# Query features turned by VectorE's 32x32 block transposes in place of TensorE transposes, in an attention-and-GLU block

## The chip, the cores and the metric

One Trainium2 chip, one of its cores. The metric is the device time of one execution in microseconds, the median of several runs. PE is TensorE (its weight loads are shown as PEld), DVE is VectorE, ACT is ScalarE, POOL is GpSimd, and SP is the queue from which this kernel issues all its DMAs. L123 is line 123 of the kernel before.

## The reference

```python
def _A_ref(x, wqkv, w_phi, wo):                 # S 2048, D 1024, H 32 heads, Dh 32
    qkv = (x @ wqkv) -> q, k, v per head
    pq = einsum("bhsd,hdf->bhsf", q, w_phi);  pk the same from k
    phi_q = concat([softmax(pq), softmax(-pq)], -1)      # 64 features a head
    phi_k = concat([softmax(pk), softmax(-pk)], -1)
    kv = einsum("bhsf,bhsd->bhfd", phi_k, v);  z = einsum("bhsf->bhf", phi_k)
    num = einsum("bhqf,bhfd->bhqd", phi_q, kv)
    den = einsum("bhqf,bhf->bhq", phi_q, z)[..., None] + 1e-6
    return (num / den) -> (B, S, D) @ wo

def _B_ref(x, w_gate, w_up, w_down):            # F 3584
    return (sigmoid(x @ w_gate) * (x @ w_up)) @ w_down

xn = layernorm(x)
return x + _A_ref(xn, ...) * silu(_B_ref(xn, ...))
```

Everything is float32.

## The kernel before

A float32 product is made of three matmuls on two-part operands: `split` (L120) copies a tile's rounded part on ACT (L122) and subtracts it on DVE (L123), and `mm3` (L125) issues the three matmuls (L127, L128, L129). Big products go through a 2x2 block scheme with seven products instead of eight; the seven are named B11, B21, T2, T3, T4, T1, B22, and their operands are sums of blocks made on POOL.

The program runs in this order: layer norm and transposes of x; the projections to v, k and q (w_phi is folded into the q and k weights by `fold`); the gate and up products of the GLU, with the key features, the key-value sums and half of the query features in their background; the GLU's down product; then attention and the output product. Token tiles have 128 rows, so there are 16 (TT); heads come in two halves of 512 columns (`hb`, HB).

The query features go through memory three times. `features` (L398) makes exp of the shifted values for both signs from one [128, 512] tile of q, so `e` is [128 tokens, 1024 features] with columns ordered head, sign, feature. For the first eight token tiles `q_features` (L554) does this early and stores `e` in `e_d` and its reciprocal sums in `r_d`; for the other eight `q_task` (L562) does it itself. `q_task` runs 32 times during the down product, popped from `late` in its loop (L926 to L931). It multiplies `e` by the broadcast key sums (POOL, L573), reduces to the denominator (DVE, L576 to L584), scales `e` in place (POOL, L585) and stores it in `e_d` again with one DMA of 512 KB (L586).

In the last stage the scaled features are needed with features on partitions. `e_load` (L612) reads one [128, 1024] tile back into slot 47 or 48 (u is 0 or 1). `phi_transpose` (L618) does four TensorE transposes of 128x128 into one PSUM bank (L623), then splits the bank into two-part operands (ACT reads the bank first, then DVE), and after the second quarter of a tile calls `e_load` for the next one. `numerator` (L632) multiplies by the key-value blocks, copies the result (ACT, L641), and `o_operands` (L648) makes the seven operands of the output product: three copies and four differences on POOL (L653, L656, L657, L661), each then split. `attend` (L665) lists for a pair of token tiles 8 `phi_transpose` and 4 `numerator` calls. Pair 0 is spread over the end of the down product; pair p+1 is spread over the 28 k-steps of pair p's output product (loop at L976), whose results leave the PSUM bank by L992 (ACT) and L994, L996, L1003, L1006 (DVE), are multiplied by the gate and added to x (POOL, L1007 and L1008), and are stored (L1009); `gx_load` (L965) then loads the next gate and x tiles (L970, L971).

The output weights are made into operands by `wo_prep` (L603): load, split, through a ring of two half slots. Those of T1, T4 and B22 come last, when the down product frees its slots.

The order of instructions on each engine is the program order as changed by a planner that follows a timeline model and by the `issue_after` blocks. All DMAs sit on SP in one order, and an SP entry that waits holds what is behind it. PSUM has eight banks: in the last stage two are for transposes (`tpr`), two for numerators (`nmr`), four for the output product (`amm`).

Of the kernel before, what the change touches and what calls it, by code (L numbers as in the profile page):

```python
# [9 lines left out]
F32 = mybir.dt.float32  # L10
F32R = mybir.dt.float32r
AF = mybir.ActivationFunctionType
ALU = mybir.AluOpType
AX = mybir.AxisListType
# [3 lines left out]
P = 128  # L18
S, D, H, DH, F = 2048, 1024, 32, 32, 3584
KT = D // P  # L20
TT = S // P
NCH = 2
CT = S // NCH
CTT = CT // P
NF = F // P
NJ = NF // 2
HB = 512
EPS_LN = 1e-5
EPS_DEN = 1e-6
Q, K, V, O = 0, 1, 2, 3  # L30
# [18 lines left out]
def hedgehog_glu_kernel(  # L49
# [11 lines left out]
    nc = tc.nc  # L61
# [4 lines left out]
    dram = ctx.enter_context(tc.tile_pool(name="dram", bufs=1, space=DRAM))  # L66

    ident = sb.tile([P, P], F32, name="ident")
# [2 lines left out]
    wf_d = dram.tile([4, 7, P, 4, HB], F32, name="wf_d")  # L71
    qkv_d = dram.tile([3, TT, 2, P, HB], F32, name="qkv_d")
    xo_d = dram.tile([7, P, 4, HB], F32, name="xo_d")
    e_d = dram.tile([TT, 2, P, 2 * HB], F32, name="e_d")
    r_d = dram.tile([CTT, 2, P, 32], F32, name="r_d")
    zb_d = dram.tile([2, P, 2 * HB], F32, name="zb_d")
    kvbd_d = dram.tile([4, P, 2, HB], F32, name="kvbd_d")
    ws_d = dram.tile([2 * NJ, 4, P, 2 * HB], F32, name="ws_d")
# [27 lines left out]
    def whole(i):  # L106
        return slots[i].rearrange("p a n -> p (a n)")

    def halves(*ids):
        return [slots[i][:, a] for i in ids for a in range(2)]  # L110

    def run(i, n):

        name, k = where[i]
        return blocks[name][0][:, k:k + n]

    def pair(i):
        return slots[i][:, 0], slots[i][:, 1]

    def split(o, src):  # L120

        nc.scalar.copy(o[0], src)  # L122
        return nc.vector.tensor_sub(o[1], src, o[0].bitcast(F32))  # L123
# [94 lines left out]
    def w_sums(which, k, a11, a12, a21, a22):  # L218
        def keep(i, b):
            nc.sync.dma_start(wf_d[which, i, :, k], b)  # L220

        if which != O:
            for i, b in ((B11, a11), (B21, a12), (T4, a22)):
                keep(i, b)
        nc.gpsimd.tensor_add(a22, a21, a22)
        nc.gpsimd.tensor_sub(a21, a11, a21)
        nc.gpsimd.tensor_sub(a11, a22, a11)
        nc.gpsimd.tensor_sub(a12, a12, a11)
        for i, b in ((T2, a11), (T3, a21), (T1, a22), (B22, a12)):
            keep(i, b)  # L230
# [29 lines left out]
    def fold(which, k):  # L260

        bs = halves(*fblock[which].next())
        for b, (f, h) in zip(bs, ((0, 0), (0, 1), (1, 0), (1, 1))):
            r = fraw.next()
            nc.sync.dma_start(r, wqkT[which, f, k + 4 * h].rearrange("p g n -> p (g n)"))
            ps = tps.next()
            for g in range(4):
                gs = slice(g * P, (g + 1) * P)
                nc.tensor.matmul(ps[:, gs], r[:, gs], bd[:, 4 * f + g], start=True, stop=True)
            nc.scalar.copy(b, ps)  # L270
        w_sums(which, k, *bs)


# [121 lines left out]
            evac(y, u1p[u])  # L395
            store(1, 0, y)

    def features(name, p, e):  # L398

        nh = HB // DH  # L400
        st = small.tile([P, 4, nh], F32, name=f"st{name}", tag="st", bufs=2)
        pv = p.rearrange("p (h d) -> p h d", d=DH)
        mx, mn = st[:, 0], st[:, 1]
        nc.vector.tensor_reduce(mx, pv, axis=AX.X, op=ALU.max)
        nc.vector.tensor_reduce(mn, pv, axis=AX.X, op=ALU.min)
        ev = e.rearrange("p (h t d) -> p h t d", t=2, d=DH)
        nc.vector.tensor_tensor(ev[:, :, 0], pv, mx[:, :, None].to_broadcast([P, nh, DH]), op=ALU.subtract)
        nc.vector.tensor_tensor(ev[:, :, 1], mn[:, :, None].to_broadcast([P, nh, DH]), pv, op=ALU.subtract)
        nc.scalar.activation(e, e, AF.Exp)  # L409
        s2, r2 = [st[:, a:a + 2].rearrange("p t h -> p (t h)") for a in (2, 0)]  # L410
        nc.vector.tensor_reduce(s2, e.rearrange("p (g d) -> p g d", d=DH), axis=AX.X, op=ALU.add)
        nc.vector.reciprocal(r2, s2)
        return r2
# [3 lines left out]
    e_k, zacc = whole(53), whole(54)  # L417
    kvb = banks[4:]
# [60 lines left out]
    def z_broadcast(hb):  # L479

        for i in range(2):
            z = zacc[:, i * HB:(i + 1) * HB]
            a = pair(38)
            split(a, z)
            nc.tensor.matmul(kvb[i], ones, a[0], start=True, stop=False)
            nc.tensor.matmul(kvb[i], ones, a[1], start=False, stop=True)
            nc.scalar.copy(z, kvb[i])
        nc.sync.dma_start(zb_d[hb], zacc)

    def x_task(t):  # L490
        xt = x_load(t, 52)
# [62 lines left out]
    def q_features(t, hb):  # L554

        p, e = qf_raw.next(), whole(qf_e.next())
        nc.sync.dma_start(p, qkv_d[Q, t, hb])
        r = features(f"q{t}{hb}", p, e)
        nc.sync.dma_start(r_d[t, hb], r)
        nc.sync.dma_start(e_d[t, hb], e)  # L560

    def q_task(t, hb):  # L562
        e, ez = whole(eqr.next()), whole(52)
        if t < CTT:
            nc.sync.dma_start(e, e_d[t, hb])
            r = small.tile([P, 32], F32, name=f"r{t}{hb}", tag="r", bufs=2)
            nc.sync.dma_start(r, r_d[t, hb])
        else:
            p = qraw.next()
            nc.sync.dma_start(p, qkv_d[Q, t, hb])  # L570
            r = features(f"q{t}{hb}", p, e)
        st = small.tile([P, 5, 16], F32, name=f"sa{t}{hb}", tag="sa", bufs=2)
        nc.gpsimd.tensor_mul(ez, e, zb)  # L573
        d2 = st[:, 0:2].rearrange("p t h -> p (t h)")
        r2 = st[:, 2:4].rearrange("p t h -> p (t h)")
        nc.vector.tensor_reduce(d2, ez.rearrange("p (g d) -> p g d", d=DH), axis=AX.X, op=ALU.add)  # L576
        nc.vector.tensor_mul(d2, d2, r)
        den = st[:, 4]
        nc.vector.tensor_reduce(den, d2.rearrange("p (h t) -> p h t", t=2), axis=AX.X, op=ALU.add)
        nc.vector.tensor_scalar_add(den, den, EPS_DEN)  # L580
        nc.vector.reciprocal(den, den)
        nc.vector.tensor_mul(r2.rearrange("p (h t) -> p h t", t=2), r.rearrange("p (h t) -> p h t", t=2),
                             den[:, :, None].to_broadcast([P, 16, 2]))
        e3 = e.rearrange("p (g d) -> p g d", d=DH)  # L584
        nc.gpsimd.tensor_mul(e3, e3, r2[:, :, None].to_broadcast([P, 32, DH]))  # L585
        nc.sync.dma_start(e_d[t, hb], e)  # L586

# [22 lines left out]
    def e_load(u):  # L612
        tp_, hb = divmod(e_next[u], 2)
        if tp_ < NTP:
            nc.sync.dma_start(whole(47 + u), e_d[2 * tp_ + u, hb])
        e_next[u] += 1

    def phi_transpose(tp_, u, hb, q):  # L618
        ps = tpr.next()
        e = whole(47 + u)  # L620
        for j in range(4):
            k = 4 * q + j
            nc.tensor.transpose(ps[:, j * P:(j + 1) * P], e[:, k * P:(k + 1) * P], ident)  # L623
        if u == 0:
            b = run(phu.next(), 2).rearrange("p a b n -> p (a b n)")
            units_ph[hb, q] = b.rearrange("p (a k t) -> p a k t", a=2, t=256)
        ph, cs = units_ph[hb, q], slice(u * P, (u + 1) * P)
        split((ph[:, 0, :, cs], ph[:, 1, :, cs]), ps.rearrange("p (k t) -> p k t", t=P))
        if q:
            e_load(u)  # L630

    def numerator(tp_, hb, q):  # L632
        ps = nmr.next()
# [96 lines left out]
    for k in range(4):  # L730
        todo(fold, K, k)
    todo(x_rest)
    for k in range(4):
        todo(fold, Q, k)
# [29 lines left out]
    for n, (kind, c, what, i) in enumerate(ops):  # L764
# [20 lines left out]
        j, s = what  # L785
        u = units.index((c, j, s))
# [29 lines left out]
        else:  # L816
            q = {B21: 0, T1: 3, T4: 2, B22: 1}[i]
            g = gates[q]
# [6 lines left out]
            else:  # L825
                if q == 0:
                    nc.vector.tensor_mul(g, g, bank)
                else:
                    b = u1 if q == 1 else u2
# [76 lines left out]
    for n, (i, j, cs) in enumerate(dsteps):  # L906
        w, hs = dready[n]
        for c in cs:
            for u in range(4):
                p = 4 * c + u  # L910
# [15 lines left out]
        if n and n * 32 // 78 > (n - 1) * 32 // 78 and late:  # L926
            t, hb = late.pop(0)
            if t == 0:
                nc.sync.dma_start(zb, zb_d[hb])
            with tc.issue_after(last_split[0]):  # L930
                q_task(t, hb)  # L931
        if 40 <= n < 56 and n % 2 == 0:
            wo_prep(*divmod((n - 40) // 2, 4))
        if n == ND - 2 * NJ:
            assert not late and len(WO[B21]) == 4
            block("x1", 4, 4, F32R)
            for i in (T3, B21):
                side.extend([lambda i=i, k=k: wo_prep(i, k) for k in range(4)])
            side.extend([lambda u=u: e_load(u) for u in range(2)])
# [21 lines left out]
    def rows(tp_, i):  # L961
        f, u = {B21: (0, 0), T1: (1, 1), T4: (1, 0), B22: (0, 1)}[i]
        return 2 * tp_ + u, slice(f * HB, (f + 1) * HB)
# [12 lines left out]
    for tp_ in range(NTP):  # L976
        nxt = attend(tp_ + 1) if tp_ + 1 < NTP else []
        n = 0
        u1, u2, y11, y21 = [res.next() for _ in range(4)]
        for i in range(7):  # L980
            if i in opening:
                abank[i] = amm.next()
            ps = abank[{B21: B11, T4: T3, B22: T1}.get(i, i)]
            o = [h.rearrange("p (k t) -> p k t", t=P) for h in pair(of[tp_][i])]
# [12 lines left out]
            else:  # L997
                g, xt = gxs.pop((tp_, i))
                t, cols = rows(tp_, i)
# [40 lines left out]
```

## Time and profile before

| | |
|---|---|
| median of 3 runs | 2444.24 us (2442.29 to 2448.07) |
| span of the profiled execution | 2442.7 us |
| PE, DVE, ACT, POOL busy, share of the span | 98%, 71%, 41%, 40% |
| mean granted clock of TensorE | 0.998 |
| DMA | 581.60 MB, mean 238 GB/s |
| first and last TensorE transpose of query features (L623) | 2150.1 us, 2408.0 us |

The profile shows one execution. Beside its span no separate time of that execution is given; the span lies 1.5 us under the median of the runs. Matmuls overlap one another, so a busy PE isn't by itself a PE at its peak: the distance from one matmul's start to the next tells what one costs. In a row of groups stand line, engine, operation, written tile and read tiles, shapes and count, then the busy time with the mean of one in ns, then the engine's idle time just before them with what ended it. In a row of waits stand who waited for whom, the total in us, the times and the longest.

### The profile page before, as it was taken

How to read it: one execution, taken by the hardware profiler on the slowest of the kernel's cores; microseconds unless marked ns; L12 is line 12 of the kernel's file. 1: busy time of each engine (PE TensorE's matmuls, PEld its weight loads, DVE VectorE, ACT ScalarE, POOL GpSimd, SP SyncE). 2: the span in 40 equal slices, each digit the busy share in tenths (PEclk: the TensorE clock that was granted, in tenths of full speed). 3: DMA queues.
4: the chain of work that ended last, by engine and by line, in shares of the span. 5: the costliest groups of instructions: out<-in, count | busy, mean ns of one | idle time of the engine just before them, and what ended most of it. 6: DMA issues, size and time to landing. Idle time of an engine off the chain costs nothing. (4 is left out here: it accounts for less than half of the span.)

```text
span 2442.7 us, 31915 instructions
## 1 busy us (share of the span) xinstructions
PE 2386.8 (98%) x11048; PEld 1979.6 (81%) x11048; DVE 1722.3 (71%) x2261; ACT 1001.9 (41%) x1495; POOL 981.5 (40%) x638
## 2 busy tenths in 40 slices
PE   6999999999999999999999999999999999998998
PEld 4888888888888888888888888888888888877887
DVE  7533567767776688548868888647889998865544
ACT  6432244444444443323433444433443334454332
POOL 4530146566665400004545453543333335314554
PEclk9999999999999999999999999999999999999999
DMA  7874567777776764467888887896666767756554
GB/s 275 278 253 169 186 225 266 251 261 263 259 273 244 259 221 167 175 202 260 285 301 286 270 312 267 280 335 216 216 225 220 241 231 241 239 193 193 182 177 130
DMA packets 231506, 581.60 MB, mean 238 GB/s; under 512 B 30385, under 2 KB 30385, under 8 KB 226737
## 3 DMA queue, kind: packets, MB, share of 16 engines
q1 hardware_dynamic: 231344, 579.57, 69.0%
q8 instruction: 87, 1.43, 0.2%
q14 instruction: 75, 0.61, 0.1%
HBM read 353.76 MB, written 225.71 MB: 237 GB/s over the span
## 5 line engine op out<-in xcount | busy, mean ns | idle before, releaser
L127 PE MATMUL bank<-x,w 128*128 128x512 f32 x2352 | 911.3, 390 | 6.8 <-DVE fb L823 2.7
L128 PE MATMUL bank<-x,w 128*128 128x512 f32 x2352 | 916.2, 390 | 0.4 <-DVE x L123 0.3
L129 PE MATMUL bank<-x,w 128*128 128x512 f32 x2352 | 904.5, 389 | 0.0
L123 DVE TENSOR_TENSOR w<-fa,w 128x512 fp32r<-128x512 f32 (+1 forms) x444 | 436.1, 987 | 143.6 <-ACT w L122 139.2
L122 ACT CAST w<-fa 128x512 fp32r<-128x512 f32 (+1 forms) x444 | 307.6, 698 | 541.7 <-PE bank L128 333.4
L127 PEld LDWEIGHTS bank<-x,w 128*128 128x128 f32 x2352 | 441.1, 188 | 101.6 <-DVE fb L823 4.1
L129 PEld LDWEIGHTS bank<-x,w 128*128 128x128 f32 x2352 | 441.6, 188 | 91.9 <-DVE w L123 0.4
L128 PEld LDWEIGHTS bank<-x,w 128*128 128x128 f32 x2352 | 441.7, 188 | 91.5 <-DVE x L123 1.4
L127 PE MATMUL bank<-w,x 128*128 128x512 f32 x708 | 279.1, 395 | 5.2 <-ACT fc L377 2.1
L129 PE MATMUL bank<-w,x 128*128 128x512 f32 x708 | 278.2, 393 | 5.8 <-DVE x L123 5.8
L128 PE MATMUL bank<-w,x 128*128 128x512 f32 x708 | 277.4, 392 | 0.0
L831 POOL TENSOR_TENSOR fc<-fc 128x512 f32<-128x512 f32 x27 | 43.2, 1599 | 298.6 <-DVE fc L830 292.6
L129 PEld LDWEIGHTS bank<-w,x 128*128 128x128 f32 x708 | 133.9, 189 | 35.4 <-DVE x L123 7.8
L127 PEld LDWEIGHTS bank<-w,x 128*128 128x128 f32 x708 | 134.0, 189 | 34.4 <-ACT x L122 3.0
L128 PEld LDWEIGHTS bank<-w,x 128*128 128x128 f32 x708 | 133.9, 189 | 27.1 <-DVE w L123 0.2
L573 POOL TENSOR_TENSOR fc<-fc 128x1024 f32<-128x1024 f32 x32 | 81.4, 2543 | 179.4 <-ACT fc L409 123.2
L831 POOL TENSOR_TENSOR fb<-fb,fc 128x512 f32<-128x512 f32 x57 | 91.7, 1608 | 133.4 <-DVE fc L830 130.4
L313 POOL TENSOR_TENSOR fb<-fa 128x512 f32<-128x512 f32 x28 | 36.7, 1309 | 249.3 <-DMA fa<-w_gu 129.6
L123 DVE TENSOR_TENSOR w<-fb,w 128x512 fp32r<-128x512 f32 (+1 forms) x114 | 107.3, 941 | 30.7 <-ACT w L122 29.4
L122 ACT CAST w<-fb 128x512 fp32r<-128x512 f32 (+1 forms) x114 | 71.4, 626 | 135.4 <-PE bank L128 90.3
L123 DVE TENSOR_TENSOR x<-fa,x 128x512 fp32r<-128x512 f32 x112 | 112.7, 1007 | 17.4 <-ACT x L122 17.1
L830 DVE TENSOR_TENSOR fc<-fc,bank 128x512 f32<-128x512 f32 x84 | 57.2, 681 | 88.5 <-PE bank L129 74.9
(240 smaller groups left out, 3293.7 us busy)
## 6 DMA issues: line engine op xcount, KB each, us to landing
ws_d<-w SPq DMA_DIRECT2D x112, 512.0 KB, 3.8
w<-ws_d SPq DMA_DIRECT2D x112, 512.0 KB, 5.6
fa<-w_gu SPq DMA_DIRECT2D x84, 512.0 KB, 4.1
fa<-h_d SPq DMA_DIRECT2D x84, 512.0 KB, 4.1
fa<-wf_d SPq DMA_DIRECT2D x32, 1024.0 KB, 5.2
h_d<-fc SPq DMA_DIRECT2D x120, 256.0 KB, 3.6
fc<-e_d SPq DMA_DIRECT2D x48, 512.0 KB, 3.8
fc<-qkv_d SPq DMA_DIRECT2D x80, 256.0 KB, 4.0
```

The lines of the kernel that those rows point to most:

```text
L122: nc.scalar.copy(o[0], src)
L123: return nc.vector.tensor_sub(o[1], src, o[0].bitcast(F32))
L127: nc.tensor.matmul(o, a[0], b[0], start=first, stop=False, **kw)
L128: nc.tensor.matmul(o, a[0], b[1], start=False, stop=False, **kw)
L129: nc.tensor.matmul(o, a[1], b[0], start=False, stop=last, **kw)
L313: nc.gpsimd.tensor_add(s1, a21, a22)
L573: nc.gpsimd.tensor_mul(ez, e, zb)
L830: v = nc.vector.tensor_add(b, u2 if q == 3 else u1, bank)
L831: nc.gpsimd.tensor_mul(g, g, b)
```

## The change

The four TensorE transposes of a quarter tile become one VectorE instruction that transposes every 32x32 block of [128, 512] inside its own quadrant of 32 partitions, from SBUF into the same PSUM bank. A block transpose leaves a block in its quadrant, so the rows that lie in one quadrant must already be one quarter of the features. This is arranged ahead of it. The store of the scaled features goes to a new tensor `f_d` in four DMAs, each from 32 partitions (32 tokens) and scattering four runs of 1 KB per partition, so that a reloaded tile has on partition (quarter of the columns, token in block) the columns (block of tokens, feature). `fold` writes the folded q weights with the heads' order changed, in the ACT copy out of PSUM; `features` writes `e` for queries in the order half, sign, head, feature; the key sums of `z_broadcast` are copied in that order too, into `e_k` instead of in place; the denominators' small operations read by the new order. `e_load` reads whole rows of `f_d`, and stands ahead of the split instead of behind it. `e_d` keeps only the early features of eight tiles.

```diff
-    e_d = dram.tile([TT, 2, P, 2 * HB], F32, name="e_d")
+    e_d = dram.tile([CTT, 2, P, 2 * HB], F32, name="e_d")
     r_d = dram.tile([CTT, 2, P, 32], F32, name="r_d")
+    f_d = dram.tile([TT, 2, 4, DH, 4, 256], F32, name="f_d")
...
@@ fold
-            nc.scalar.copy(b, ps)
+            if which == Q:
+                nc.scalar.copy(b.rearrange("p (a g d) -> p g a d", a=2, d=DH), ps.rearrange("p (g a d) -> p g a d", a=2, d=DH))
+            else:
+                nc.scalar.copy(b, ps)
...
@@ features
-        ev = e.rearrange("p (h t d) -> p h t d", t=2, d=DH)
-        nc.vector.tensor_tensor(ev[:, :, 0], pv, mx[:, :, None].to_broadcast([P, nh, DH]), op=ALU.subtract)
-        nc.vector.tensor_tensor(ev[:, :, 1], mn[:, :, None].to_broadcast([P, nh, DH]), pv, op=ALU.subtract)
+        if query:
+            ev = e.rearrange("p (a t h d) -> p t a h d", a=2, t=2, d=DH)
+            pv, mx, mn = [a.rearrange("p (a h) d -> p a h d", a=2) for a in
+                          (pv, mx[:, :, None].to_broadcast([P, nh, DH]), mn[:, :, None].to_broadcast([P, nh, DH]))]
+        else:
+            ev = e.rearrange("p (h t d) -> p t h d", t=2, d=DH)
+            mx, mn = [a[:, :, None].to_broadcast([P, nh, DH]) for a in (mx, mn)]
+        nc.vector.tensor_tensor(ev[:, 0], pv, mx, op=ALU.subtract)
+        nc.vector.tensor_tensor(ev[:, 1], mn, pv, op=ALU.subtract)
...
@@ z_broadcast
-            nc.scalar.copy(z, kvb[i])
-        nc.sync.dma_start(zb_d[hb], zacc)
+            o = e_k.rearrange("p (q g d) -> p g q d", q=4, d=DH)[:, 4 * i:4 * i + 4]
+            nc.scalar.copy(o, kvb[i].rearrange("p (g q d) -> p g q d", q=4, d=DH))
+        nc.sync.dma_start(zb_d[hb], e_k)
...
@@ q_task (the small operations on d2, den and r2 read by "p (a t h) -> p a h t")
-        nc.sync.dma_start(e_d[t, hb], e)
+        for n in range(4):
+            nc.sync.dma_start(f_d[t, hb, :, :, n].rearrange("q s c -> s q c"),
+                              e[n * DH:(n + 1) * DH].rearrange("s (q c) -> s q c", q=4))
...
@@ e_load
-            nc.sync.dma_start(whole(47 + u), e_d[2 * tp_ + u, hb])
+            nc.sync.dma_start(whole(47 + u), f_d[2 * tp_ + u, hb].rearrange("q s n c -> (q s) (n c)"))
@@ phi_transpose
-        e = whole(47 + u)
-        for j in range(4):
-            k = 4 * q + j
-            nc.tensor.transpose(ps[:, j * P:(j + 1) * P], e[:, k * P:(k + 1) * P], ident)
+        nc.vector.transpose(ps.rearrange("p (g n s) -> p n g s", n=4, s=DH),
+                            whole(47 + u).rearrange("p (n g d) -> p n g d", n=4, d=DH)[:, :, 4 * q:4 * q + 4])
+        if q:
+            e_load(u)
         if u == 0:
...
         split((ph[:, 0, :, cs], ph[:, 1, :, cs]), ps.rearrange("p (k t) -> p k t", t=P))
-        if q:
-            e_load(u)
```

More of the change, by code (lines that the diff above doesn't have):

```diff
@@ L396, in proj_out, with features @@
             store(1, 0, y)
-    def features(name, p, e):
+    def features(name, p, e, query=False):
         nh = HB // DH
@@ L557, in q_features @@
         nc.sync.dma_start(p, qkv_d[Q, t, hb])
-        r = features(f"q{t}{hb}", p, e)
+        r = features(f"q{t}{hb}", p, e, True)
         nc.sync.dma_start(r_d[t, hb], r)
@@ L570, in q_task @@
             nc.sync.dma_start(p, qkv_d[Q, t, hb])
-            r = features(f"q{t}{hb}", p, e)
+            r = features(f"q{t}{hb}", p, e, True)
         st = small.tile([P, 5, 16], F32, name=f"sa{t}{hb}", tag="sa", bufs=2)
@@ L578, in q_task @@
         den = st[:, 4]
-        nc.vector.tensor_reduce(den, d2.rearrange("p (h t) -> p h t", t=2), axis=AX.X, op=ALU.add)
+        by_head = "p (a t h) -> p a h t"
+        nc.vector.tensor_reduce(den.rearrange("p (a h) -> p a h", a=2), d2.rearrange(by_head, a=2, t=2), axis=AX.X, op=ALU.add)
         nc.vector.tensor_scalar_add(den, den, EPS_DEN)
         nc.vector.reciprocal(den, den)
-        nc.vector.tensor_mul(r2.rearrange("p (h t) -> p h t", t=2), r.rearrange("p (h t) -> p h t", t=2),
-                             den[:, :, None].to_broadcast([P, 16, 2]))
+        nc.vector.tensor_mul(r2.rearrange(by_head, a=2, t=2), r.rearrange(by_head, a=2, t=2),
+                             den.rearrange("p (a h) -> p a h", a=2)[:, :, :, None].to_broadcast([P, 2, 8, 2]))
         e3 = e.rearrange("p (g d) -> p g d", d=DH)
         nc.gpsimd.tensor_mul(e3, e3, r2[:, :, None].to_broadcast([P, 32, DH]))
-        nc.sync.dma_start(e_d[t, hb], e)
+        for n in range(4):
+            nc.sync.dma_start(f_d[t, hb, :, :, n].rearrange("q s c -> s q c"),
+                              e[n * DH:(n + 1) * DH].rearrange("s (q c) -> s q c", q=4))
     NTP = TT // 2
```

## The prediction

> **What bounds the kernel now.** I read the page's busy shares first (in the table above: PE far ahead of all others), then busy time by stretch around the transposes, then PE's timeline for what one transpose costs, then the waits. The stretches are A, the end of the down product (pair 0 is turned there); B, from there until the last output weights are ready; C, the loop over the pairs. The last pair follows, without transposes. Columns: length, then busy us of PE, PEld, DVE, ACT, POOL, granted clock, DMA share, GB/s. The second fence is the same table for the transposes' line alone, L623.
>
> ```profile
> 2142.00:2183.00 41.00, 37.83 (x197) 31.07 (x196) 29.52 (x42) 24.04 (x44) 7.20 (x5) 1.00 0.77 255
> 2183.00:2242.00 59.00, 52.12 (x268) 42.17 (x266) 33.52 (x45) 24.85 (x46) 19.94 (x15) 1.00 0.47 146
> 2242.00:2415.00 173.00, 169.75 (x968) 146.04 (x969) 89.16 (x122) 64.27 (x116) 90.34 (x66) 1.00 0.55 177
> ```
> ```profile
> 2142.00:2183.00 41.00, 4.94 (x32) 3.87 (x32) 1.00 0.77 255
> 2183.00:2242.00 59.00, 5.37 (x40) 4.61 (x40) 1.00 0.47 146
> 2242.00:2415.00 173.00, 26.51 (x184) 21.94 (x184) 1.00 0.55 177
> ```
>
> In C PE is busy 169.75 of 173 us at full clock and DVE only 89.16, so PE is the bound there and DVE has half its time free. A and B leave PE idle 3.2 and 6.9 us: something else sets their pace in part. The 256 transposes lie 32, 40 and 184 in A, B and C.
>
> PE's timeline shows a group of four between ordinary 128x512 matmuls:
>
> ```profile
> 2161.12 0.39 PE L128 MATMUL bank<-x,w 128*128 128x512 f32 x1
> 2161.35 0.60 PE L623 MATMUL bank<-ident,fc 128*128 128x128 f32 x4
> 2161.71 0.48 PE L129 MATMUL bank<-x,w 128*128 128x512 f32 x1
> 2162.02 0.40 PE L127 MATMUL bank<-x,w 128*128 128x512 f32 x1
> ```
>
> A matmul normally starts 0.23 us after the one before it (2161.12 to 2161.35). From the group's start to the second matmul behind it is 0.67 us (2161.35 to 2162.02); less one matmul, a group costs 0.44 us of PE.
>
> **The change, part by part.**
>
> *TensorE loses 64 groups:* 64 x 0.44 = 28.2 us of PE time: 8 groups or 3.5 us in A, 10 or 4.4 us in B, 46 or 20.2 us in C. In C it is on the path. In B I count little: PE waits there for operands, and the chain of waits runs through the output weights (load, ACT, DVE, next load), then the load of a gate:
>
> ```profile
> 2222.19 4.82 DMA fc<-wf_d
> 2227.03 0.63 ACT x L122
> 2227.68 0.70 DVE x L123
> 2228.40 3.73 DMA fc<-wf_d
> ...
> 2233.53 3.16 DMA fc<-g_d
> ```
>
> None of this gets shorter, so of B's 4.4 us I take 1. In A I take 0: the operands of the down product pass through DVE, whose 29.52 busy us of 41 grow by eight transposes, and PE already stands idle 3.2 us.
>
> *VectorE gains 64 transposes of 128x512.* The profile has none. The nearest rows are other DVE work of 512 float32 per lane:
>
> ```profile
> L123 DVE TENSOR_TENSOR fb<-bank,fb 128x512 fp32r<-128x512 f32 x32 | 21.9, 685 | 27.5 <-ACT fb L122 27.4
> ...
> L404 DVE TENSOR_REDUCE stk<-fc 128x16 f32<-128x512 f32 x32 | 21.6, 676 | 0.2 <-DMA fc<-qkv_d 0.2
> ...
> L407 DVE TENSOR_TENSOR p<-p,stq 128x512 f32<-128x512 f32 x16 | 22.5, 1408 | 0.0
> ...
> L432 DVE COPY fc<-fc 128x1024 f32<-128x1024 f32 x2 | 2.5, 1234 | 0.0
> ```
>
> The lower end is half the copy of twice the length, 0.62 us; the upper is the slowest row of this shape, 1.41 us. I take 0.69 us: a transpose has one SBUF source, like the reduce at 0.68, and writes as many elements. Then DVE has 89.2 + 46 x 0.69 = 120.9 us in C, which shrinks to about 157: 77% busy, not the bound. In A it has 29.5 + 5.5 = 35.0 of 41.
> [...] No run here shows a transpose on DVE.
>
> *The price of the in-order queue.* DVE now does the transposes ahead of the splits that PE waits for. PE's waits in C:
>
> ```profile
> PE bank L127 <- ACT fa L122: 1.7, 1, 1.7
> PE bank L127 <- ACT fc L992: 1.3, 1, 1.3
> PE bank L623 <- DVE x L123: 0.9, 2, 0.5
> PE bank L129 <- DVE x L123: 0.8, 2, 0.4
> ```
>
> Two of the four are already splits late at the seam between two pairs. I charge one transpose, 0.69 us, at each of six seams: 4.1 us. A load of `e` that comes late would now hold DVE instead of PE, with the evacuations (L994 to L1006) and splits queued behind it; today transposes on PE wait for splits (0.9 us above), not for a load, so I charge nothing more. SP's entry for that load waits for the transpose as before (47.4 us in total, below), and what is behind it (gate loads, output stores) moves with it; moved ahead of the split, it costs nothing.
>
> *The stores.* 32 stores become 128, so SP gets 96 more issues of 0.32 us, 31 us over the 420 us of the stores. The load of a later `e` waits on SP for them:
>
> ```profile
> SPq L615 <- PE bank L623: 47.4, 15, 9.1
> ```
> ```profile
> L586 SPq DMA_DIRECT2D e_d<-fc x32: 319/320/659, 1677.5 to 2095.8; - x32
> ...
> DMA to landing us min/median/max: 2.6/3.9/6.4
> ```
> ```profile
> SPq L565 <- DMA e_d<-fc: 42.5, 15, 4.1
> ```
> ```profile
> ACT x L122 <- DMA fa<-wd_d: 31.5, 15, 5.7
> ```
> ```profile
> PE bank L127 <- DVE fc L895: 0.6, 1, 0.6
> PE bank L127 <- DVE x L890: 0.6, 1, 0.6
> ```
>
> Behind that load stand the down product's own loads, and ACT already waits 31.5 us for them, yet the last two rows are all the waits of PE from 1640 to 2142 us. The prepared steps cover it, so I take 0. Without that cover, one more microsecond a store is 15 us.
>
> *The rest at nothing.* The 16 ACT copies in `fold` (0.586 us each by the next row) write in another order; ACT is idle half the time there. If each doubled, 9.4 us would lie on ACT beside PE. The views in `features`, the denominator and the key sums keep counts and sizes.
>
> ```profile
> L270 ACT COPY fc<-bank x16: 576/586/593, 94.8 to 148.5; 128x512 f32<-128x512 f32 x16
> ```
>
> *Sum:* 0 (A) - 1 (B) - 20.2 + 4.1 (C) = -17.1 us. From the span 2442.7 that is 2425.6; the median of the runs stands 1.5 us above the span, so 2427.
>
> **The rivals.**
>
> *All of it is on the path.* PE's waits move elsewhere and A and B shrink too: 28.2 us, 2416. For it: PE is busy 98% of C. Against it: A and B have idle PE while they wait for loads.
>
> *The pairs keep their pace.* If the loop over pairs is set by a result's way out (DVE, POOL, store, then the copy L992 into the same buffer), a lighter PE only waits longer:
>
> ```profile
> 2330.48 0.59 ACT L992 COPY fc<-bank 128x512 f32<-128x512 f32 x1 [2.29 <-DMA out<-fc]
> ...
> 2388.79 0.59 ACT L992 COPY fc<-bank 128x512 f32<-128x512 f32 x1 [0.61 <-DMA out<-fc]
> ```
>
> Of seven such copies only these two show a wait today, and the first costs PE 1.3 us. If the 3.4 us that PE saves a pair is mostly lost here, 15 us of C's go and 2440 is left. Against it: the other five.
>
> *VectorE becomes the bound (slower).* In C this decides when 89.2 + 46X passes 173, at X = 1.82 us. At 2.2 us it is 190: +17 us, 2461. Against it: no row of this shape is above 1.41 us.
>
> *The stores are late (slower).* Each leaves from 32 partitions in 1 KB runs. If the landing doubles by 3.9 us, SP holds the down product's loads 15 x 3.9 = 59 us longer; with half of it uncovered the time is 2427 + 29 = 2456. It decides once the prepared steps run out, after some 17 us uncovered. Against it: 31.5 us of late loads cost PE 1.2.
> [...]
>
> **How the numbers follow.** No change means within 0.2%, 4.9 us, about what a measurement of this kernel can tell. Chances: forecast (2420 to 2434) 0.56; all on the path (2414 to 2419) 0.14; pairs keep their pace (2435 to 2446) 0.20, half of it faster and half the same; VectorE the bound 0.06; late stores 0.04. Faster 0.56 + 0.14 + 0.10 = 0.80, same 0.10, slower 0.10. The range 2414 to 2444 leaves out the two slower cases and the end of the third, some 0.14.
>
> **What would show it.** Right: no L623 on PE; 64 DVE transposes near 0.69 us; about 157 us in place of C's 173; A and B within 2 us of before; PE still over 95% busy in C; PE from 1640 to 2142 us without new waits. Wrong: a transpose above 1.2 us, PE waiting for DVE or L992 for several us a pair, or waits of PE on loads in the down product.

## The result, and the profile after

| | before | changed |
|---|---|---|
| median of four runs | 2445.88 us (2442.29 to 2448.07) | 2428.65 us (2427.05 to 2428.80) |
| span of the profiled execution | 2442.7 us | 2426.7 us |

The ratio is 0.9927, with a 95% interval of 0.9913 to 0.9941: 17.2 us faster. The forecast was 2427. That the sum came out to 2 us is partly luck: the last stage gained more than was forecast and the stages ahead of it lost time, by about the same amount, as the following shows. In the kernel after, the old lines L122/L123 (split), L127 to L129 (matmuls), L586 (store), L615 (load of `e`), L641, L901, L992 and L994 are L123/L124, L128 to L130, L599, L629, L653, L913, L1004 and L1006; the block transpose is L634.

The page of the changed kernel, engines and DMA packets (231506 packets and 30385 under 2 KB before):

```profile
PE 2364.4 (97%) x10792; PEld 1957.0 (81%) x10792; DVE 1752.7 (72%) x2325; ACT 999.1 (41%) x1495; POOL 982.7 (40%) x638
...
DMA packets 245329, 581.59 MB, mean 240 GB/s; under 512 B 31920, under 2 KB 48304, under 8 KB 240560
```

The new group of instructions on DVE, with its mean in ns and the idle time before it:

```profile
L634 DVE STREAM_TRANSPOSE bank<-fc 128x512 f32<-128x512 f32 x64 | 45.7, 716 | 5.6 <-DMA fc<-f_d 5.1
```

Busy time by stretch of the last stage, columns as in the prediction: first from 2242 us, where C starts there, past the last transpose (2388.9 us), then two pieces of it. The second fence has the same piece of the kernel before.

```profile
2242.00:2400.00 158.00, 151.05 (x772) 127.60 (x771) 118.33 (x166) 61.73 (x114) 93.42 (x65) 0.98 0.58 186
...
2250.00:2270.00 20.00, 14.60 (x70) 12.11 (x70) 15.90 (x23) 9.99 (x19) 9.46 (x8) 0.83 0.53 163
2270.00:2330.00 60.00, 59.38 (x306) 50.73 (x305) 42.51 (x60) 19.80 (x38) 39.77 (x29) 1.00 0.67 217
```
```profile
2270.00:2330.00 60.00, 58.95 (x337) 50.37 (x335) 32.10 (x44) 21.98 (x40) 32.24 (x24) 1.00 0.55 179
```

PE is as full as before (59.38 of 60 us) but now with ordinary matmuls only, and DVE has room left (42.51). The weak spot is 2250 to 2270, where the granted clock falls to 0.83 and PE stands idle for 5.4 us.

Where the time went is read best from two anchors that both kernels have: the last sum of the gate and up products on DVE (here the form that ends last, L827 before and L839 after), and the sums of the down product's last block product (L901 and L913). Each row ends with its first and last start; before, then after:

```profile
L827 DVE TENSOR_TENSOR fb<-fb,bank x19: 628/678/689, 329.7 to 1638.2; 128x512 f32<-128x512 f32 x19
...
L901 DVE TENSOR_TENSOR x<-x,bank x8: 678/679/682, 2148.4 to 2201.5; 128x512 f32<-128x512 f32 x8
```
```profile
L839 DVE TENSOR_TENSOR fb<-fb,bank x19: 627/677/689, 331.0 to 1644.4; 128x512 f32<-128x512 f32 x19
...
L913 DVE TENSOR_TENSOR x<-x,bank x8: 666/668/681, 2158.1 to 2210.4; 128x512 f32<-128x512 f32 x8
```

Starts are compared (each sum itself takes 0.7 us or less):

| us | before | changed | difference |
|---|---|---|---|
| up to the end of the gate and up products | 1638.2 | 1644.4 | +6.2 |
| from there to the first sum of the last down product ("down product" below) | 510.2 | 513.7 | +3.5 |
| its eight sums | 53.1 | 52.3 | -0.8 |
| from its last sum to the end ("last stage" below) | 241.2 | 216.3 | -24.9 |
| span | 2442.7 | 2426.7 | -16.0 |

So the last stage gained more than the 17.1 us of the forecast, and 9.7 us were lost ahead of it (8.9 with the sums' 0.8 taken off), where the forecast had zero. There is one trace of the kernel before, so its stage lengths are those of a single execution; e1 below, which turns on TensorE too, has the same last stage (241.3 us). PE's waits show little of this loss: from 1640 to 2142 us they are now

```profile
PE bank L128 <- DVE x L902: 1.4, 2, 0.9
PE bank L128 <- DVE fc L907: 1.0, 1, 1.0
PE bank L130 <- DVE w L124: 0.4, 1, 0.4
```

which is 2.8 us against 1.2. From 2200 us to the end, where no single wait was longer than 2.5 us before, the three largest are

```profile
PE bank L128 <- ACT fc L1004: 4.8, 6, 2.1
PE bank L128 <- ACT w L123: 3.6, 1, 3.6
PE bank L128 <- ACT fb L123: 2.9, 1, 2.9
```

and behind the first of them stands the result's way out, in all engines' waits of the same stretch:

```profile
DVE fc L1006 <- ACT fc L1004: 24.2, 6, 6.9
ACT fc L1004 <- DMA out<-fc: 20.8, 6, 6.5
```

Before, the copy L992 waited for a store twice (2.29 and 0.61 us). Now it does so six times, 20.8 us, with DVE's sum behind it; only 4.8 us of it reach PE directly, which has four banks for the output product.

### The profile page after: what moved, and what is told of

Read it like the earlier page. It is cut to its first block, busy times and chain, and to the rows that moved or that the text cites. A ratio compares the mean times of both kernels' runs of the same rounds, so it can differ in the third digit from the quotient of the medians.

```text
span 2426.7 us, 31652 instructions
## 1 busy us (share of the span) xinstructions
PE 2364.4 (97%) x10792; PEld 1957.0 (81%) x10792; DVE 1752.7 (72%) x2325; ACT 999.1 (41%) x1495; POOL 982.7 (40%) x638
## 4 chain that ended last, share of the span: by engine, by line
PE 68%; DVE 10%; DMA 9%; issue 6%; POOL 4%; ACT 2%; SPq 1%; POOLq 0%; ACTq 0%; DVEq 0%
PE bank L128 22%; PE bank L129 22%; PE bank L130 22%; DVE x L124 2%; DVE w L124 2%; DMA fa<-w_down 1%; DMA w<-ws_d 1%; PE bank L454 1%; DMA fb<-w_down 1%; POOL fc L1020 1%; DMA fc<-wo 1%; DMA f_d<-fc 1%; POOL fc L1019 1%; DMA wf_d<-x 1%; ACT x L123 1%
## 5 line engine op out<-in xcount | busy, mean ns | idle before, releaser
L128 PE MATMUL bank<-x,w 128*128 128x512 f32 x2352 | 911.1, 391 | 9.5 <-DVE fb L835 2.9
L129 PE MATMUL bank<-x,w 128*128 128x512 f32 x2352 | 917.1, 390 | 2.3 <-DVE x L124 2.2
L130 PE MATMUL bank<-x,w 128*128 128x512 f32 x2352 | 904.5, 389 | 0.4 <-DVE w L124 0.4
L124 DVE TENSOR_TENSOR w<-fa,w 128x512 fp32r<-128x512 f32 (+1 forms) x444 | 436.7, 989 | 140.5 <-ACT w L123 139.0
L123 ACT CAST w<-fa 128x512 fp32r<-128x512 f32 (+1 forms) x444 | 307.9, 698 | 547.4 <-PE bank L129 337.5
L128 PEld LDWEIGHTS bank<-x,w 128*128 128x128 f32 x2352 | 441.3, 188 | 105.9 <-DVE fb L835 4.3
L129 PEld LDWEIGHTS bank<-x,w 128*128 128x128 f32 x2352 | 442.1, 188 | 95.0 <-DVE x L124 4.8
L130 PEld LDWEIGHTS bank<-x,w 128*128 128x128 f32 x2352 | 442.0, 188 | 92.5 <-DVE w L124 0.9
L128 PE MATMUL bank<-w,x 128*128 128x512 f32 x708 | 279.3, 395 | 8.0 <-ACT w L123 3.6
L130 PE MATMUL bank<-w,x 128*128 128x512 f32 x708 | 278.1, 394 | 6.1 <-DVE x L124 6.1
L129 PE MATMUL bank<-w,x 128*128 128x512 f32 x708 | 278.3, 393 | 0.0
L128 PEld LDWEIGHTS bank<-w,x 128*128 128x128 f32 x708 | 134.1, 189 | 38.3 <-ACT w L123 4.3
L130 PEld LDWEIGHTS bank<-w,x 128*128 128x128 f32 x708 | 134.3, 190 | 35.2 <-DVE x L124 7.7
L129 PEld LDWEIGHTS bank<-w,x 128*128 128x128 f32 x708 | 134.3, 190 | 27.1
L124 DVE TENSOR_TENSOR w<-fb,w 128x512 fp32r<-128x512 f32 (+1 forms) x114 | 107.0, 939 | 30.7 <-ACT w L123 23.9
L123 ACT CAST w<-fb 128x512 fp32r<-128x512 f32 (+1 forms) x114 | 71.4, 626 | 135.4 <-PE bank L129 98.7
L124 DVE TENSOR_TENSOR x<-fa,x 128x512 fp32r<-128x512 f32 x112 | 109.5, 979 | 18.0 <-ACT x L123 18.0
```

The lines of the kernel that those rows point to most:

```text
L128: nc.tensor.matmul(o, a[0], b[0], start=first, stop=False, **kw)
L129: nc.tensor.matmul(o, a[0], b[1], start=False, stop=False, **kw)
L130: nc.tensor.matmul(o, a[1], b[0], start=False, stop=last, **kw)
```

## The experiments

The question is whether the gain is PE's lighter load in the last stage, nearly all of it, with the rest of the change (stores, orders, key sums) costing some microseconds in the down product, or whether the forecast's sum holds as it stood, with the seams taking part of the gain and the rest costing nothing. Each expectation says what it sets against what. Each time below stands beside the kernel before on the same chip; the changed kernel is 17.2 us under it in the runs above and 21.1 us under it in a second set (e5), so differences of 2 or 3 us between variants are not told from such a spread by the medians alone. For that the stages of the profiled executions are used.

**The change in its two halves.** e1 keeps the whole change but turns the tile with four TensorE transposes again; e2 is the kernel before with only the transposes given to DVE.

```diff
 e1 (on the changed kernel)
-        nc.vector.transpose(ps.rearrange(...), whole(47 + u).rearrange(...)[:, :, 4 * q:4 * q + 4])
+        e = whole(47 + u)
+        for j in range(4):
+            k = 4 * q + j
+            nc.tensor.transpose(ps[:, j * P:(j + 1) * P], e[:, k * P:(k + 1) * P], ident)
 e2 (on the kernel before): the reverse
```

In e1, e2 and e3 the tile is turned in another way than it was stored, so what they compute is another output; the work and the shapes are those named. e2 also leaves the next load of `e` behind the split, as before.

> The changed kernel with the four TensorE transposes put back in place of the VectorE one; stores, head order and key sums stay changed, so the blocks that it turns are not the ones that the product needs and the output is another. Theory 1: the rest of the change costs the 9 us by which the changed kernel's profile reaches the end of the down product later, so this is 9 us above the kernel before, about 2455 us. Rival: the rest costs nothing and those 9 us are the spread from one execution to the next, so this stays within 4 us of the kernel before, about 2446 us.

> The kernel before with only the VectorE transpose in place of the four TensorE ones; one store of 512 KB, old order of heads, old key sums, so the output is another. Theory 1 (the rest costs 9 us): 2420 us, 9 us under the changed kernel, and 25 us or more under the kernel before. Rival (the rest costs nothing): 2429 us, like the changed kernel. Either way the 64 transposes take about 0.72 us each and the stage from the last evacuation of the down product to the end lasts 216 us as in the changed kernel, not 241.

e1: 2451.51 us, ratio 1.0025 (1.0016 to 1.0034), 6.2 us slower than before. e2: 2422.78, ratio 0.9901 (0.9886 to 0.9916), 22.5 us faster. e1 lies between its two expectations, e2 near its theory. Together they are -16.3; the change gave -17.2 and, in the second set, -21.1. So the halves add within that spread. In stages, e1 keeps the old last stage (241.3 us) and has a longer down product (515.6); e2 has the new last stage (219.7) and a short down product (508.8). The gain is the turning, the loss is the rest. (e1's profiled execution, 2454.89 us, is 3.4 us above its median, so its stages are rather too long.)

**Which part of the rest.** e3 stores a tile with one DMA of 128 partitions instead of four; e4 takes the key sums back to their old place; e5 is the changed kernel unaltered; e6 stores once and scatters at the load instead, with four loads into 32 partitions each.

```diff
 e3
-        for n in range(4):
-            nc.sync.dma_start(f_d[t, hb, :, :, n].rearrange("q s c -> s q c"), e[n * DH:(n + 1) * DH].rearrange(...))
+        nc.sync.dma_start(f_d[t, hb].rearrange("q s n c -> (q s) (n c)"), e)
 e4
-            nc.scalar.copy(o, kvb[i].rearrange("p (g q d) -> p g q d", q=4, d=DH))
-        nc.sync.dma_start(zb_d[hb], e_k)
+            nc.scalar.copy(z, kvb[i])
+        nc.sync.dma_start(zb_d[hb], zacc)
 e6
+        nc.sync.dma_start(f_d[t, hb], e)
 ... and in e_load
+        for n in range(4):
+            nc.sync.dma_start(whole(47 + u)[n * DH:(n + 1) * DH].rearrange("s (n c) -> s n c", n=4),
+                              f_d[2 * tp_ + u, hb, :, n * 256:(n + 1) * 256].rearrange("(n s) c -> s n c", s=DH))
```

> The changed kernel with one contiguous store of 512 KB in place of the four scattering ones; the reloaded tiles are in another order, so the output is another. If the stores cost the 3 us that the down product lost: 2426 us and PE's waits in the down product back to about 1.2 us. If they are covered: 2429 us, with the waits as before or after within the spread.

> The changed kernel with the key sums copied back in place and in the old order, as in the kernel before, so the output is another. If the copy into e_k, which the key features of the next half wait for, costs the 6 us that the GLU stage lost: 2423 us and the down product's first evacuation near 1720 us. If not: 2429 us and near 1726 us.

> The changed kernel itself once more, as the measure for the runs beside it. 2428 us if the chip makes no difference; if it comes out near 2424, then the 4 us by which the versions with one store and with the old key sums were faster came from the chip and not from their edits.

> The changed kernel with the same reordering done by the load: one contiguous store of 512 KB in the down product, and in the last stage four loads that each fill 32 partitions with runs of 1 KB. If the scattering stores cost the down product some 4 us because the transfers behind them are late, this gets back 4 us, about 2424 us, and the down product (last product of the GLU to last evacuation) lasts some 510 us, not 514. Rival: the cost moves with the scatter, since VectorE then waits for the late loads; 2429 us or more, with waits of VectorE on f_d well above the 5.1 us of the changed kernel.

| | median, us | ratio (95%) | to before | down product | last stage |
|---|---|---|---|---|---|
| e3 | 2424.13 | 0.9912 (0.9896 to 0.9929) | -21.2 | 510.5 | 217.3 |
| e4 | 2424.65 | 0.9909 (0.9894 to 0.9924) | -20.6 | 513.0 | 216.0 |
| e5 | 2426.57 | 0.9915 (0.9901 to 0.9930) | -21.1 | 511.6 | 218.8 |
| e6 | 2430.60 | 0.9930 (0.9915 to 0.9944) | -17.0 | 509.7 | 222.2 |

By the medians e3, e4 and e5 are one kernel; a gain of any of them over the change isn't shown. The key sums' copy is not what the first stage lost: e3 keeps it and e4 doesn't, and on one chip their last gate and up sums start at 1640.3 and 1640.1 us. The stages say a little more. All nine profiled kernels that scatter on SP during the down product (after, e1, e4, e5 and e8 to e13 below) take 510.8 to 515.6 us for it, mean 512.8; the four that don't (before, e2, e3, e6) take 508.8 to 510.5, mean 509.8. The two groups all but touch (510.5 and 510.8), and each number is one execution; e3 and e4, on one chip, differ by 2.5, e6 and e5 on another by 1.9. So the scattering stores cost some 2 to 3 us there, 0.1 us a tile, not nothing and not the 29 us of the rival. With them POOL gets a new wait, 13.6 to 13.9 us in three times on a store of `f_d` (after, e1, e4, e5; none in before, e3, e6); that it is what reaches PE isn't shown. In e6 both expectations came true in part: the down product has its 509.7 us, and the cost has moved. The last stage is 3.4 us longer than e5's (222.2 against 218.8), DVE, which now turns the tile, waits 15.4 us for loads of `e` (e5: 5.3), and PE 10.1 us for the result's copy (e5: 6.1). The transposes and PE's first wait in e6:

```profile
L634 DVE STREAM_TRANSPOSE bank<-fc 128x512 f32<-128x512 f32 x64 | 45.9, 717 | 19.7 <-DMA fc<-f_d 15.4 <-DMA fc<-x 3.7
```
```profile
PE bank L128 <- ACT fc L1004: 10.1, 5, 4.8
```

**What DVE's time costs.** e8 and e9 do each transpose twice and three times, into the same bank. The planner places the extra instructions like all others, so a shift in the order is part of what they measure.

```diff
         nc.vector.transpose(ps.rearrange(...), whole(47 + u).rearrange(...)[:, :, 4 * q:4 * q + 4])
+        nc.vector.transpose(ps.rearrange(...), whole(47 + u).rearrange(...)[:, :, 4 * q:4 * q + 4])   # e8; e9 once more
```

> The changed kernel with every VectorE transpose done twice, 1.43 us a quarter in place of 0.72. The prediction's sum for VectorE (89.2 us of other work in the loop over the pairs, 46 transposes) gives 155 us against some 153 us of PE work: just at the bound. If the transpose is hidden up to there, the time rises by no more than the seams' charge, 0.7 us a pair, 5 us: 2434 us. Rival: the in-order queue makes every transpose late work for PE, and most of 64 x 0.72 = 46 us shows: above 2455 us.

> The changed kernel with every VectorE transpose done three times, 2.15 us a quarter. By the same sum VectorE has 89.2 + 46 x 2.15 = 188 us in the loop over the pairs, so it is the bound there and loses 35 us against the changed kernel's 153, with some 10 more where the down product ends: 2465 to 2475 us, above the kernel before. Rival: the bound is elsewhere and the time stays under the kernel before, 2446 us.

e8: 2448.08 us, ratio 1.0003 (0.9993 to 1.0012), 21.5 us over e5. e9: 2465.63, ratio 1.0078 (1.0061 to 1.0095), 39.1 over e5. The extra DVE time is about 45 us for each repetition (64 times 0.70). e8 missed both of the values that were expected, and lies between them; e9 falls within 2465 to 2475. In e8 DVE is busy 45.63 us of 60 and 53.22 of 70, then in e9 55.59 of 60:

```profile
2270.00:2330.00 60.00, 55.30 (x276) 45.70 (x274) 45.63 (x70) 19.02 (x35) 30.95 (x22) 0.97 0.55 172
2330.00:2400.00 70.00, 60.37 (x291) 50.08 (x292) 53.22 (x81) 25.20 (x48) 35.93 (x27) 0.93 0.57 181
```
```profile
2270.00:2330.00 60.00, 51.56 (x253) 42.94 (x252) 55.59 (x85) 21.10 (x38) 29.69 (x22) 0.94 0.55 172
```

So half of an added DVE microsecond shows in the time with DVE no more than 76% busy. The changed kernel has 71% and 76% in these pieces (42.51 of 60, 53.15 of 70): e8's added work made the stage longer and DVE hardly fuller. What stands behind it in e8 are waits of DVE for its load (22.8 us; 5.1 in the changed kernel) and of PE for the result's copy; in e9 PE waits for operands. Which of them carries the price isn't separated, and a slower granted clock, 0.97 and 0.93 in e8's rows and 1.00 in e5's of the same pieces, stands beside them. PE's and DVE's waits from 2200 us on, e8, then e9:

```profile
DVE bank L634 <- DMA fc<-f_d: 22.8, 14, 4.6
...
PE bank L128 <- ACT fc L1006: 11.4, 6, 3.6
PE bank L128 <- ACT fa L123: 5.1, 2, 3.8
```
```profile
PE bank L128 <- ACT x L123: 17.9, 7, 4.1
PE bank L128 <- ACT fa L123: 10.6, 3, 6.0
```

**The stores from ACT's queue.** If SP's 96 more issues were the price, another queue would take it away.

```diff
-            nc.sync.dma_start(f_d[t, hb, :, :, n]...
+            nc.scalar.dma_start(f_d[t, hb, :, :, n]...
```

> The changed kernel with the four scattering stores issued from ACT's queue instead of SP's. If their cost in the down product (some 4 us) comes from SP, where the loads of the down product stand behind them, it is gone: 2423 us, the stretch from the last product of the GLU to the first evacuation of the down product's last product near 510 us instead of 514. Rival: ACT, which makes half of every split, now waits for POOL at the head of its queue, and the time is 2427 us or more.

2446.85 us, ratio 0.9999 (0.9989 to 1.0009): the whole gain is gone, 16 to 20 us. The rival came true, at far more than it asked. The down product takes 530.9 us. ACT's queue now holds the four stores behind POOL's product, and the split behind the stores, as one place of the timeline shows: POOL ends at 1730.25 us, the issues follow at once, and ACT has idled 5.30 us before its split:

```profile
1727.98 2.27 POOL L597 TENSOR_TENSOR fc<-fc,sa 128x1024 f32<-128x1024 f32 x1 [1.10 <-DVE sa L594]
1730.29 1.94 ACTq L599 DMA_DIRECT2D f_d<-fc  x4
1732.27 0.62 ACT L123 CAST w<-fa 128x512 fp32r<-128x512 f32 x1 [5.30 <-PE bank L130]
```

The releaser named there, a matmul, is not the last thing that ended. In the waits of ACT from 1640 to 2140 us much of the idle time is now put down to the issue and to the store; in the changed kernel the issue has 31.0 us and no split waits for a store. PE gets the longest wait of its down product from it: at 1966.65 us ACT's split starts behind four stores that waited for POOL, DVE's half and a sum (L904) follow, and PE starts at 1970.53:


```profile
ACT w L123 <- issue: 47.2, 12, 8.2
...
ACT x L123 <- issue: 36.5, 7, 8.0
...
ACT x L123 <- DMA f_d<-fc: 28.1, 4, 10.8
```
```profile
PE bank L128 <- DVE x L904: 6.2, 1, 6.2
```

From SP these stores cost the down product some 2 to 3 us; from ACT's queue, where the splits stand behind them and their wait for POOL, they cost 16 to 20 us more.

**What holds the last stage now.** Two waits of the changed kernel are left: the last output weights, which go through two half slots one at a time, and the result buffers, of which the next pair takes first the one that was stored last. They are seen in e5 (2195 to 2270 us, and from 2200 us to the end):

```profile
ACT w L123 <- DMA fc<-wf_d: 12.9, 3, 9.2
...
PE bank L128 <- ACT w L123: 3.4, 2, 3.1
...
ACT fc L1004 <- DMA out<-fc: 28.7, 7, 6.8
DVE fc L1006 <- ACT fc L1004: 25.1, 6, 6.3
```

e10 gives the ring of the last output weights two more half slots, those of the key sums' slot 54, free by then; e12 lets the four result buffers rotate, so that a pair starts in the buffers that the pair before did not store last; e13 does both.

```diff
 e10, where the down product's last block product frees its slots (n == ND - 2 * NJ)
+                wor.items = halves(53, 54)
 e12
+    bufs = [res.next() for _ in range(4)]          # ahead of the loop over the pairs
     ...
-        u1, u2, y11, y21 = [res.next() for _ in range(4)]
+        u1, u2, y11, y21 = bufs
+        bufs = [y11, y21, u2, u1]
```

> The changed kernel with four half slots instead of two for the loads of the last output weights, from the point where the key sums' slot is free. If the two stalls of PE at the start of the loop over the pairs (3.1 and 2.9 us in the repeated run of the changed kernel, with 13.7 us of halved clock behind them) hang on that chain of loads: 8 to 12 us less, 2415 to 2419 us. Rival: the gate loads and the splits hold the same place anyway: 2427 us.

> The changed kernel with the four result buffers taken in another order in the next pair, so that the copy L1004 writes the buffer that was stored first and not the one that was stored last. Theory: the pairs' pace hangs on that copy (28.7 us of waits for the store, 6.1 us of them PE's, in the repeated run of the changed kernel): 5 to 8 us less, 2419 to 2422 us, and the waits of L1004 for stores near 0. Rival: PE's next wait (late splits) stands right behind it: 2426 us.

> The changed kernel with both, the four half slots for the last output weights and the result buffers in another order. If the two remove different waits, the gains add (10.3 and 7.6 us under the repeated run of the changed kernel, 2426.57): 2409 us, between 2406 and 2412. Rival: both had removed the same idle time at the start of the loop over the pairs, and the time stays at 2416 us.

| | median, us | ratio (95%) | to before | last stage |
|---|---|---|---|---|
| e5 (the change) | 2426.57 | 0.9915 (0.9901 to 0.9930) | -21.1 | 218.8 |
| e10 | 2416.24 | 0.9873 (0.9854 to 0.9891) | -31.8 | 209.7 |
| e12 | 2419.00 | 0.9883 (0.9862 to 0.9903) | -29.1 | 207.3 |
| e13 | 2406.91 | 0.9833 (0.9816 to 0.9849) | -40.7 | 200.6 |

e10 and e12 gain 10.7 and 8.0 us beyond the change, and together 19.6; all three medians lie in the ranges that were expected. The planner also orders the stage anew: in e12 the second pair's copy into its first result buffer starts 20 us behind the first pair's, in e5 46, so its gain is that of the buffers with this order. e13 beats both kernels. PE in two pieces of its last stage, and all of its longer waits from 2200 us on:

```profile
2250.00:2310.00 60.00, 57.97 (x301) 49.32 (x300) 51.67 (x70) 26.96 (x50) 40.32 (x28) 1.00 0.66 209
2310.00:2380.00 70.00, 70.00 (x373) 60.30 (x372) 55.53 (x75) 29.18 (x53) 43.45 (x31) 1.00 0.61 193
```
```profile
PE bank L128 <- ACT w L123: 2.1, 1, 2.1
PE bank L128 <- DVE fc L1021: 0.8, 1, 0.8
PE bank L128 <- ACT x L123: 0.7, 1, 0.7
```

The wait of PE on the copy into the result buffer is gone, and the granted clock is 1.00 there.

## Why the prediction was right, and where it was not

*64 groups at 0.44 us, 28.2 us of PE.* Right. In the trace before, 54 of them (23.8 us) start behind the down product's last sum and ten (4.4 us) ahead of it; the last stage gave 24.9 in the changed kernel, 21.5 in e2, 22.4 in e5.

*A at nothing.* Right as a length, wrong as a reason. The ten groups stand among the eight sums, and this stretch lasts 53.1 us before, 52.3 in the changed kernel and 52.5 in e2. But it holds more work. PE's counts of matmuls, before and after:

```profile
2148.40:2201.50 53.10, 48.60 (x254) 40.42 (x253) 37.33 (x51) 28.53 (x51) 12.06 (x9) 1.00 0.55 184
```
```profile
2158.10:2210.40 52.30, 49.79 (x245) 40.92 (x245) 43.52 (x68) 29.08 (x55) 11.22 (x8) 1.00 0.64 215
```

Of the 254, 40 are transposes, so 31 more matmuls of products run there now: 21 of 256 columns, 0.12 us apart, and 10 of 512, 0.23 us apart, some 4.8 us of work that stood behind the last sum before. So A's transposes did pay, and what they paid shows in the last stage, which could now gain 23.8 + 4.8 us. e2 has 245 there too, e1 254 like the kernel before.

*B at 1, C at 20.2 less 4.1 for the seams.* This is the first term that was mis-sized: with A at nothing 17.1 us were taken, and 21.5 to 25.2 measured (e2, e3, e4, e5 and the changed kernel). A's share is part of the error. The charge of one transpose at each of six seams is another: behind 2270 us PE waits 2.6 us in all, every time for the result's copy. At the start of the stage PE does wait for splits, 3.6 us for an output weight, 1.4 for another operand and 2.9 and 0.3 for turned features. The 2.9 us are the case for which the prediction charged nothing more, a late load of `e` that holds DVE: the load is issued at 2250.05 us, behind two gate loads; DVE waits 1.86 us for it, ACT's split 4.01 and PE 2.94 (2257.13). How much of the error is B's and how much C's isn't separated, since product work crossed the borders. That B's chain of loads was on the path is right: e10, which shortens it, gains 10.7 us more, and in it the wait for the weight is 1.9 us and the one for the features is gone.

*The stores at nothing.* The second mis-sized term: some 2 to 3 us in the down product (e3 and e6 against the others). An issue takes 0.43 us, not 0.32, so SP has some 45 us more of them and not 31. The cover that the prediction named would explain why so little shows: the landing is 2.9 us for a store of a quarter of the bytes, and ACT's waits for the down product's loads stayed where they were (31.8 us against 31.5). SP's line of the stores and that wait:

```profile
L599 SPq DMA_DIRECT2D f_d<-fc x128: 303/430/1003, 1683.8 to 2105.8; - x128
...
DMA to landing us min/median/max: 2.0/2.9/5.0
```
```profile
ACT x L123 <- DMA fa<-wd_d: 31.8, 18, 4.1
```

A store of 128 KB from 32 partitions took 2.9 us from issue to landing, one of 512 KB from 128 partitions in e3 3.8, so by the byte the small one took some three times as long. No run here takes apart what of that is the 32 partitions and what the size of the store or its 1 KB runs. That the landing could double, on which the rival's 2456 rests, was the author's estimate, and no run shows it: a store landed in 3.9 us before and lands in 2.9 now.

*The remainder at nothing.* Of the 9.7 us lost ahead of the last stage, 6.2 lie before 1644.4 us, and no edit is shown to cause them. e2 changes nothing there and reaches that point at 1641.3, e3 at 1640.3, e4 at 1640.1, the others at 1641.1 to 1644.7; the one execution of before at 1638.2 is the earliest of all. Part of it is therefore spread of single executions, and some of that has a name: a stall between 1550 and 1555 us is followed by matmuls at half pace, worth about 1.6 us, in the changed kernel and in all others that come at 1641.3 or later, but not in before, e3, e4 and e10 (1638.2, 1640.3, 1640.1, 1641.1); the last section shows it. e1's median, 6.2 us over before with 2 to 3 of them in the stores, leaves room for some 3 us that stay open.

*A transpose at 0.69 us.* Measured 0.716. The reason that was given is weak, since the reduce beside which it was set writes 16 elements per partition and not 512; that the price came so near is partly luck. By a straight line from e5 to e8 (21.5 us for 0.69 us more a quarter) each 0.1 us more a quarter would have cost some 3 us of the gain, an estimate. e2, the turn alone, gains 22.5 us, since PE is the bound in the loop over the pairs (169.75 of 173 us busy before) and DVE isn't (89.16). e2 leaves out the arranging that a block transpose needs; with it the change still gains 17 to 21 us.

*VectorE the bound from 1.82 us.* Here a step failed, though the forecast came out: DVE's time was taken as free until DVE is full. e8, with 1.41 us a quarter, is already level with before (ratio 1.0003), and DVE isn't full in it (76% busy); about half of the added time is on the path. In e9, at 93%, DVE is nearly full. In the changed kernel itself DVE is busy 118.33 of 158 us, 75%, where 77% was forecast.

*The pairs keep their pace.* The place was right and the price too high. The copy waits 20.8 us for the store, and PE 4.8 for the copy; e12, which removes this wait, gains 8.0 us, so it cost about that, not the 15 of the rival (whose 2440 is 2442 by its own sum, 2427 + 15).

*What would show it.* L623 is gone and 64 transposes are there. The 158 us of the stretch in the result do not prove the 157 that were given, since it starts at 2242 us in both kernels: the last output weight's load is issued at 2228.40 us before and at 2240.51 now, the last transpose starts at 2407.9 and 2388.9, so from the one to the other it is 179.5 and 148.4 us. PE is 95.6% busy in it (151.05 of 158), just above the 95% named; 5.4 of the 6.95 us that are missing lie between 2250 and 2270. "No new waits of PE" in the down product was wrong by 1.6 us.

## What to carry to other kernels

Moving work off the bounding engine gave most of what that engine spent on it, start to start (17 to 21 us of 28.2 here), and part of the gain showed in another stage than the one it was taken from, because work moved up into the free time. The price is to be looked for where the data are arranged for the new engine, and in the engine that takes the work: its time was not free before it was full (e8: 21.5 us more, with DVE 76% busy). After such a gain, the waits that grew behind the lighter engine (here a result buffer and a ring of two half slots) were worth nearly as much again (19.6 us).

## What the hardware showed beyond that

A short stall of PE can be followed by a stretch of slow matmuls. After 2.38 us without work, matmuls in the changed kernel start 0.43 us apart for 3.3 us (1555.77 to 1559.10), not 0.23. In the kernel before, the same place has a stall of 1.94 us, and the pace stays. But the length doesn't decide it: in e3 the same place has 2.38 us again, and the pace stays too. The changed kernel, before, and e3:

```profile
1554.65 0.50 PE L128 MATMUL bank<-x,w 128*128 128x512 f32 x1 [2.38 <-DVE fb L835]
...
1555.77 0.63 PE L129 MATMUL bank<-x,w 128*128 128x512 f32 x1
1556.19 0.63 PE L130 MATMUL bank<-x,w 128*128 128x512 f32 x1
...
1559.10 0.39 PE L129 MATMUL bank<-x,w 128*128 128x512 f32 x1
```
```profile
1550.00 0.50 PE L127 MATMUL bank<-x,w 128*128 128x512 f32 x1 [1.94 <-DVE fb L823]
1550.34 0.40 PE L128 MATMUL bank<-x,w 128*128 128x512 f32 x1
```
```profile
1552.17 0.50 PE L128 MATMUL bank<-x,w 128*128 128x512 f32 x1 [2.38 <-DVE fb L833]
1552.51 0.39 PE L129 MATMUL bank<-x,w 128*128 128x512 f32 x1
1552.74 0.40 PE L130 MATMUL bank<-x,w 128*128 128x512 f32 x1
```

Elsewhere a stall of 1.86 us was followed by it (e10 at 2217.56 us: 0.43 us apart from 2218.39 to 2221.59), and one of 3.25 us was not (e2 at 2222.48, granted clock 1.00 from 2222 to 2229).

The granted clock is 0.52 from 1555.77 to 1559.10 us in the changed kernel, and 1.00 from 1550 to 1560 us in the kernel before. Such a stretch lies in the 0.83 from 2250 to 2270 us too: PE starts at 2257.13 us after 2.94 us without work, and from 2259 to 2265 us the clock is 0.50, with matmuls 0.43 us apart from 2263.05 to 2265.18. What decides whether a stall is followed by such a stretch, and how long it lasts, no run here was made to show.
